# Dummy matmuls ahead of the first products, the first gate sum behind 40 of them, and a planner with longer DMA turns and a cold tensor clock

## The chip, the cores and the metric

The kernel runs on one core of a Trainium2 chip. The metric is the time of one execution in device microseconds. On one chip the runs of one kernel spread by one or two per cent (the kernel before: 189.54 to 192.09 us on the chip of the first experiments, 186.75 to 189.81 on that of the others), and two chips differ as well: its medians there were 191.5 and 188.7 us. Kernels are therefore compared as ratios to the kernel before of the same rounds on the same chip. A ratio is the mean time of one kernel's fast runs over that of the other's, with a 95% interval, so it is not quite the ratio of the medians that are quoted.

## The reference

```
def _attn_ref(q, k, v, f_logit):           # 4 batches, 8 heads, 768 steps, 48 wide
    f = 1.0 / (1.0 + np.exp(-f_logit))
    for t in range(S):
        state = f[:, :, t, :, None] * state + np.einsum('bhd,bhe->bhde', k[:, :, t], v[:, :, t])
        y[:, :, t] = np.einsum('bhd,bhde->bhe', q[:, :, t], state)

def _moe_ref(x, w_in, w_out):              # 3072 tokens, 384 -> 2048 -> 384
    h = x @ w_in
    g = h * np.cos(h)
    return g @ w_out
```

The rows of y, 3072 tokens by 384, are the x of the second part.

## The kernel before

The recurrence is cut into 24 chunks of 128 tokens. For each chunk four loads bring f, k, q and v. ACT makes the logarithm of the gate (sp), PE sums it over the chunk (the "gate sum"), ACT takes two exponentials of the sum (b and bi), DVE or POOL multiplies them into q and k (qk), PE or a DMA transposes the product (qkt), PE forms scores, DVE masks them (am), PE forms y, y is transposed to xT, and then the products with w_in, a cosine on ACT, a multiply on DVE and the output products with w_out follow.

All operations are put into a fixed order by a small planner that runs when the program is built. Each engine then works through its own list strictly in order. The planner's estimates (durations, priorities, turns of the DMA) decide only the order; at run time semaphores decide the times.

```
def chunk_load(b, c, prio):
    for pool, src in ((fS, f_logit), (kS, k), (qS, q), (vS, v)):
        way = QUEUES[min(b * NCH + c, len(QUEUES) - 1)][len(vals)]
        eng, dma = {"S": ({"SP": 650.0}, nc.sync), "A": ({"ACT": 600.0}, nc.scalar), ...}[way]
        P.op(eng, lambda e, ...: dma.dma_start(out=t.ap, in_=ap), writes=[t], ...)
...
P.op({"PE": 268.0}, pe, reads=[sp], writes=[pc], ...)        # the gate sum
P.op({"ACT": 385.0}, ex, reads=[pc], writes=[bt], ...)       # its two exponentials
P.op({"ACT": 385.0}, lambda e, ...: ex(e, pc, bi, 1.0, H * D), reads=[pc], writes=[bi], ...)
...
order = P.run()                                              # the plan
for o in order:
    o.fn(o.eng)                                              # the program, in that order
```

A load with the letter A is issued by ACT.

Of the kernel before, what the change touches and what calls it, by code (L numbers as in the profile page):

```python
# [96 lines left out]
class Plan:  # L97


    SEM = 80.0  # L100
    DMA = 1.048
    WAIT = {'PE': 0.0, 'ACT': 196.0, 'DVE': 108.0, 'POOL': 601.0}
    RING = 2600.0

    def __init__(self):
        self.ops = []
# [34 lines left out]
    def run(self):  # L141
        engs = ("PE", "ACT", "DVE", "POOL", "SP")
        free = dict.fromkeys(engs, 600.0)
        table, lock = "E", None

        ring, large = [0.0, 0.0], False
        left = {}
        for o in self.ops:
            o.waiting = len(o.deps)
            for d in o.deps:  # L150
                d.after.append(o)
            if o.grp is not None:
                left[o.grp] = left.get(o.grp, 0) + 1
        ready = [o for o in self.ops if not o.waiting]
        order = []
        n = len(self.ops)
        while len(order) < n:
            picks, first = [], {}
            for o in ready:
                at = max([d.end + (0.0 if e0 == d.eng == "PE" else self.SEM)  # L160
                          for d in o.deps for e0 in (next(iter(o.eng)),)], default=0.0)
                ok, took = True, []
                for v in o.alloc:
                    if v.slot is not None:
                        continue
                    b = v.pool.best()
                    if b is None:
                        ok = False
                        break
                    at = max(at, b[0] + self.SEM)  # L170
                    v.pool.take(b[1])
                    took.append((v.pool, b[1]))
                for pool, i in took:
                    pool.drop(i)
                if not ok:
                    continue
                pick = None
                for e, cost in o.eng.items():
                    if e == "ACT" and lock is not None and o.grp != lock and o.table is not None:
                        continue  # L180
                    s = max(at, free[e])
                    if o.dma and e != "POOL":
                        s = max(s, ring[0] - self.RING)
                    sw = 1300.0 if e == "ACT" and o.table not in (None, table) else 0.0
                    if pick is None or s + cost + sw < pick[0]:
                        pick = (s + cost + sw, s, e, cost)
                if pick is None:
                    continue
                picks.append((o.prio, o.seq, pick[1], o, pick[2], pick[3]))
                first[pick[2]] = min(first.get(pick[2], pick[1]), pick[1])  # L190

            best = {}
            for p in sorted(picks, key=lambda p: p[:2]):
                if p[4] not in best and p[2] <= first[p[4]] + self.WAIT.get(p[4], 0.0):
                    best[p[4]] = p
            assert best, "no op can be placed: " + str(
                [(o.seq, o.eng, o.prio, lock, o.grp, [v.pool.name for v in o.alloc]) for o in ready])
            _, _, s, o, e, cost = min(best.values(), key=lambda p: (p[2],) + p[:2])
            if e == "ACT" and o.table is not None:
                if o.table != table:  # L200
                    s += 1300.0
                table = o.table
                if o.grp is not None:
                    left[o.grp] -= 1
                    lock = o.grp if left[o.grp] else None
            for v in o.alloc:
                if v.slot is not None:
                    continue
                _, i = v.pool.best()
                v.slot = i  # L210
                v.pool.take(i)
            o.start, o.end = s, s + cost + o.lat
            if o.dma:
                q = int(e == "POOL")
                o.dma *= self.DMA
                t = max(ring[q], s + cost)
                both = max(0.0, ring[1 - q] - t)
                if q:
                    large = o.dma > 1500.0
                rate = (0.96 if q else 0.18) if large else 0.6  # L220
                if o.dma <= rate * both:
                    both = o.dma / rate
                    ring[q] = t + both
                else:
                    ring[q] = t + both + o.dma - rate * both
                ring[1 - q] += both * (1.0 - (0.18 if q else 0.96)) if large else 0.4 * both
                o.end = ring[q] + o.lat
            free[e] = s + cost
            o.eng, o.cost = e, cost
            if o.frees is not None:  # L230
                pool, i = o.frees
                pool.used(i, o.end)
                pool.drop(i)
            for v in o.vals:
                v.uses -= 1
                v.pool.used(v.slot, o.end)
                if not v.uses:
                    v.pool.drop(v.slot)
            ready.remove(o)
            for a in o.after:  # L240
                a.waiting -= 1
                if not a.waiting:
                    ready.append(a)
            order.append(o)
        order.sort(key=lambda o: (o.start, o.seq))
        return order
# [3 lines left out]
def kernel(  # L250
# [21 lines left out]


    GROUPS = [1, 1, 1, 1, 1, 1, 1, 1, 2, 2, 1, 1, 2, 3, 3, 1, 1]
    UNITS = [128, 128, 128, 128, 256, 128, 128, 128, 128, 256, 128, 128, 256, 256, 128, 128, 128, 128, 256]
    ATT = [31.5, -12.35, -0.91, -97.87, -9.39, -48.94, 43.41, -95.96, -1.09, -74.7, -11.15, -52.89, 4.11, -36.04, -25.81, 1.58, -156.13, -98.92, -140.35, -95.04, -72.72, -54.06, -183.38, -29.59]
    DEC = [10.57, -49.08, 3.05, 3.32, -36.4, -43.88, -42.65, -26.96, -17.74, -34.58, -18.58, -36.54, 0.15, -26.89, -9.76, -17.28, -17.13, -64.08, -49.12, -67.43, -2.25, -59.6, -104.93, -80.41]
    MM1 = [6.06, -27.94, -32.4, -100.05, -29.46, -56.23, -91.16, -82.46, -137.1, -25.66, -11.55, -122.15, -148.98, -96.28, -109.44, -65.59, -19.47, -6.91, 25.44, -46.31, -33.1, -47.12, -85.39, 1.66]
    MM2 = [13.76, 8.41, -13.19, 54.53, -13.62, -73.77, 64.32, 9.83, 51.7, 10.46, -31.46, 0.13, 11.13, 53.52, 21.21, 60.26, 109.18, 29.72, -36.43, 48.48, -26.47, -47.8, -64.39, -82.23]

    GATES = [2, 1, 1, 2, 2, 1, 2, 2]

    QUEUES = ["AAAS", "SAAA", "SSSS", "SSSS", "SSSS", "SSSS", "SSSS"]

    QK_DMA = [7, 10, 11, 12, 14, 15, 16, 17, 18, 19, 20, 21, 22, 23]
    X_DMA = [4, 7, 11, 12, 13, 14, 16, 19, 20, 21, 22]
    FAST = 16
    WARM = 0
    BUFS = {"ld": 8, "vb": 6, "sp": 6, "b": 6, "bi": 4, "qk": 5, "qkt": 7, "am": 5, "sz": 4, "y": 4, "st": 2, "co": 5, "ot": 5, "g": 4}
    CAPS = [6, 4, 3, 3, 3]  # L290

    cpool = ctx.enter_context(tc.tile_pool(name="const", bufs=1))
# [41 lines left out]
    phS = Banks(base, "ph", CAPS[1], [moe_cap])  # L334
# [7 lines left out]
    P = Plan()  # L342
# [4 lines left out]
    mk = Val()  # L347
    P.op({"POOL": 1100.0}, masks, writes=[mk], prio=-1.0)


    warm = Val(phS)
    for i in range(WARM):
        def idle(e):
            for _ in range(2):
                nc.tensor.matmul(warm.ap[:, 0:128], lhsT=ident, rhs=ident, start=True, stop=True)
        P.op({"PE": 220.0 if i < 16 else 112.0}, idle, reads=[mk], writes=[warm], prio=1e6)
    for pool, cost in zeroed:
        for i in range(len(pool.aps)):
            P.zero(pool, i, {"DVE": cost, "POOL": 2.0 * cost}, lambda e, t=pool.aps[i]: (
# [45 lines left out]
    def decay_group(chunks, g, prio):  # L405

        outs = []
        for (b, c, ld) in chunks:
            f = ld[0]
            sp = Val(spS)  # L410
# [13 lines left out]
        for (b, c, ld, sp) in outs:  # L424
            pc, bt, bi = Val(miS), Val(bS), Val(biS)
# [6 lines left out]
                                     lhsT=sp.ap[:, 2 * p:2 * p + 2, :].rearrange("p h d -> p (h d)"),  # L432
                                     rhs=umask[:, C - 1:C], start=False, stop=(p == NP - 1))

            P.op({"PE": 268.0}, pe, reads=[sp], writes=[pc], prio=prio, lat=170.0)

            def ex(e, pc=pc, o=bt, s=-1.0, n=H * D + NP):
                nc.scalar.activation(out=o.ap, in_=pc.ap[:, 0:n], func=AF.Exp, scale=s)  # L438
# [3 lines left out]
                 reads=[pc], writes=[bi], prio=prio, table="E", grp=g)  # L442
# [3 lines left out]
    def attend(b, c, ld, bt, bi, prio):  # L446
# [3 lines left out]
        qk = Val(qkS)  # L450
        half = lambda a, i: a[:, i * NP * C:(i + 1) * NP * C].rearrange(
            "p (h d) -> p h d", d=64)[:, :, 0:D]
        qtd = qk.part(lambda a: half(a, 0))
        ktd = qk.part(lambda a: half(a, 1))
        fast = tok < FAST * C
        E = lambda e: nc.vector if e == "DVE" else nc.gpsimd
        for src, w, dst in ((qf, bt, qtd), (kf, bi, ktd)):
# [7 lines left out]
             reads=[v32], writes=[vf], prio=prio)  # L465
# [24 lines left out]
                P.op({"DVE": 340.0, "ACT": 480.0}, evac, reads=[pqk], writes=[dst], prio=prio)  # L490
        else:
            P.op({"SP": 1000.0}, lambda e: nc.sync.dma_start_transpose(out=qkt.ap, in_=qk.ap),
                 reads=[qtd, ktd], writes=[qdt, kdt], prio=prio, lat=1250.0, dma=1400.0)


        pas, ams = [Val(paS), Val(paS)], [Val(amS), Val(amS)]
# [80 lines left out]
                 prio=prio)  # L577
        else:
            P.op({"SP": 700.0}, lambda e: nc.sync.dma_start_transpose(out=x.ap, in_=yt.ap),
                 reads=[yt], writes=[x], prio=prio, lat=1250.0, dma=480.0)  # L580


    def moe(u, t0, T):
# [113 lines left out]
```

## Time and profile before

| | before |
|---|---|
| median of the first 3 timed runs, us | 191.31 (190.42 to 191.63) |
| the profiled run, us (span) | 195.14 (193.4), slow |
| PE busy, share of the span | 172.3 us, 89% |

The prediction below shows and reads the page. The columns of the timeline are start, length, engine, line, operation, and in brackets the idle time just before with what ended it; "ACTq" is ACT's instruction queue.

```profile
8.32 0.52 ACT L416 ACTIVATE sp<-f 128x384 bf16<-128x384 f32 x1
9.89 0.49 ACT L438 ACTIVATE b<-ps 128x388 f32<-128x388 f32 x1 [1.05 <-PE ps L431]
10.28 0.48 ACT L438 ACTIVATE bi<-ps 128x384 f32<-128x384 f32 x1
10.94 0.38 ACTq L400 DMA_DIRECT2D v<-in_v_dram  x1
11.37 0.52 ACT L413 ACTIVATE f<-f 128x384 f32<-128x384 f32 x1 [0.60 <-DMA q<-in_q_dram]
```

The reader is to see that the second chunk's v load is issued by ACT at 10.94, after the exponentials of the second gate sum (L438), and that ACT stands idle for 0.6 us only.

### The profile page before, as it was taken

The numbers are of one execution on the slowest core, as the hardware profiler recorded it, in microseconds if no ns is written. First come the engines' busy times: TensorE is split into PE (matmuls) and PEld (weight loads), VectorE is DVE, ScalarE is ACT, GpSimd is POOL, SyncE is SP. The second block draws the span as 40 slices with busy tenths as digits, with TensorE's granted clock in tenths as the row PEclk, the third lists the DMA queues.
The fourth block names the chain that finished last, engine by engine and source line by source line (L and its number), as shares of the span: only waits on it lengthen the run. The fifth ranks groups of instructions, "written<-read, shape, count | busy, mean of one in ns | idle before, by whom it ended". The sixth has DMA issues, their size and how long they took to land.

```text
span 193.4 us, 5275 instructions
## 1 busy us (share of the span) xinstructions
PE 172.3 (89%) x2079; PEld 135.7 (70%) x2079; DVE 135.1 (70%) x254; ACT 139.8 (72%) x257; POOL 56.7 (29%) x97
## 2 busy tenths in 40 slices
PE   0378699999999999999499999969999999999991
PEld 0256599856886897866379666955879688987750
DVE  7287879936789996989837973956349948955200
ACT  3576589595999888989948399827879899735320
POOL 7007970112130331301140119810395183000000
PEclk9999789999999999999969999979999999999999
DMA  6999999969899799998796996997989666101041
GB/s 136 219 218 197 217 203 208 192 125 233 159 190 219 174 197 204 173 185 193 163 196 131 202 221 125 184 182 155 256 183 184 228 116 135 33 0 45 1 162 43
DMA packets 124858, 31.84 MB, mean 165 GB/s; under 512 B 119713, under 2 KB 124321, under 8 KB 124833
## 3 DMA queue, kind: packets, MB, share of 16 engines
q1 hardware_dynamic: 116416, 27.18, 70.7%
q0 software_dynamic: 2176, 3.15, 9.1%
q10 hardware_dynamic: 6240, 1.18, 3.7%
q8 instruction: 16, 0.26, 0.6%
q14 instruction: 10, 0.07, 0.2%
HBM read 25.17 MB, written 4.72 MB: 155 GB/s over the span
## 4 chain that ended last, share of the span: by engine, by line
PE 65%; DMA 13%; ACT 8%; DVE 5%; POOL 3%; issue 2%; SPq 2%; ACTq 1%; POOLq 0%
PE ps L598 26%; PE ps L620 24%; DMA qkt<-qk 5%; PE ps L501 4%; DVE gT L610 3%; DMA k<-in_k_dram 3%; PE ps L482 3%; DMA v<-in_v_dram 2%; DMA xT<-y 2%; PE ps L552 2%; PE ps L520 2%; PE ps L555 2%; PE ps L428 2%; SPq L400 1%; PE ps L573 1%
## 5 line engine op out<-in xcount | busy, mean ns | idle before, releaser
L598 PE MATMUL ps<-xT,w_in 128*128 128x128 bf16 (+1 forms) x912 | 73.3, 240 | 3.5 <-DMA xT<-y 3.1
L598 PEld LDWEIGHTS <-w_in 128*128 128x128 bf16 x912 | 67.6, 116 | 6.9 <-issue 3.3
L610 DVE TENSOR_TENSOR gT<-ps,cosh 128x512 bf16<-128x512 f32 x96 | 60.4, 683 | 14.9 <-ACT cosh L606 14.6
L620 PE MATMUL ps<-w_out,gT 128*128 128x384 bf16 x384 | 70.8, 328 | 0.0
L606 ACT ACTIVATE cosh<-ps 128x512 bf16<-128x512 f32 x96 | 54.5, 602 | 21.5 <-PE ps L598 18.7
L620 PEld LDWEIGHTS <-gT 128*128 128x128 bf16 x384 | 35.1, 98 | 19.8 <-issue 0.3
L508 DVE TENSOR_TENSOR am<-ps,umask 128x512 bf16<-128x512 f32 x48 | 30.6, 682 | 6.5 <-PE ps L501 6.2
L464 POOL CAST vb<-v 128x384 bf16<-128x384 f32 x24 | 13.1, 549 | 61.2 <-DMA v<-in_v_dram 37.0
L539 POOL TENSOR_TENSOR sz<-st,b 64x192 bf16<-64x192 f32 x32 | 16.1, 502 | 16.7 <-DVE st L535 13.9
L459 POOL TENSOR_TENSOR qk<-q,b 128x384 bf16<-128x384 f32 x12 | 12.1, 1005 | 26.1 <-ACT b L438 17.1
L535 DVE TENSOR_TENSOR st<-ps,sz 64x192 f32<-64x192 f32 x32 | 11.3, 353 | 9.3 <-PE ps L520 4.4
L438 ACT ACTIVATE b<-ps 128x388 f32<-128x388 f32 x24 | 11.9, 496 | 5.7 <-PE ps L431 4.4
L629 ACT COPY ot<-ps 128x384 f32<-128x384 f32 x19 | 9.0, 485 | 8.4 <-PE ps L620 8.1
L413 ACT ACTIVATE f<-f 128x384 f32<-128x384 f32 x24 | 12.5, 522 | 2.0 <-DMA f<-in_f_logit_dram 1.3
L428 PE MATMUL ps<-sp,umask 128*128 128x384 bf16 x24 | 8.4, 355 | 5.8 <-ACT sp L416 5.7
L562 ACT CAST y<-ps 128x384 bf16<-128x384 f32 x18 | 8.5, 478 | 6.9 <-PE ps L555 5.5
L416 ACT ACTIVATE sp<-f 128x384 bf16<-128x384 f32 x24 | 12.6, 524 | 0.7
L482 PE MATMUL ps<-ident,qk 128*128 128x128 bf16 x80 | 8.3, 246 | 4.9 <-DVE qk L459 4.9
L501 PE MATMUL ps<-qkt 48*128 48x128 bf16 x192 | 10.3, 233 | 2.1 <-DMA qkt<-qk 2.0
L459 DVE TENSOR_TENSOR qk<-k,bi 128x384 bf16<-128x384 f32 x16 | 9.8, 612 | 3.2 <-ACT bi L438 3.0
L438 ACT ACTIVATE bi<-ps 128x384 f32<-128x384 f32 x24 | 11.8, 493 | 0.0
L431 PEld LDWEIGHTS <-sp 128*128 128x128 bf16 x96 | 6.1, 100 | 6.6 <-issue 4.8
(39 smaller groups left out, 139.4 us busy)
## 6 DMA issues: line engine op xcount, KB each, us to landing
out_dram<-ot SPq DMA_DIRECT2D x24, 192.0 KB, 2.7
v<-in_v_dram SPq DMA_DIRECT2D x23, 192.0 KB, 4.6
f<-in_f_logit_dram SPq DMA_DIRECT2D x23, 192.0 KB, 4.2
k<-in_k_dram SPq DMA_DIRECT2D x22, 192.0 KB, 3.9
q<-in_q_dram SPq DMA_DIRECT2D x22, 192.0 KB, 4.5
w_in<-in_moe_w_in_dram POOLq DMA_DIRECT2D x4, 384.0 KB, 7.5
w_out<-in_moe_w_out_dram POOLq DMA_DIRECT2D x4, 384.0 KB, 10.4
k<-in_k_dram ACTq DMA_DIRECT2D x2, 192.0 KB, 5.3
```

The costliest lines, as they stand in the source:

```text
L416: nc.scalar.activation(out=sp.ap[:, :, 0:D], in_=f.ap, func=AF.Ln, bias=1.0)
L438: nc.scalar.activation(out=o.ap, in_=pc.ap[:, 0:n], func=AF.Exp, scale=s)
L459: lambda e, src=src, w=w, dst=dst: E(e).tensor_mul(out=dst.ap, in0=src.ap, in1=w.ap[:, 0:H * D].rearrange("p (h d) -> p h d", d=D)),
L464: o = P.op({"POOL": 510.0}, lambda e: nc.gpsimd.tensor_copy(out=vf.ap, in_=v32.ap), reads=[v32], writes=[vf], prio=prio)
L482: nc.tensor.transpose(out=o[:, i, :], in_=qk.ap[:, j * C:(j + 1) * C], identity=ident)
L501: nc.tensor.matmul(pas[g].ap[:, p * C:(p + 1) * C], lhsT=kdt.ap[64 * g:64 * g + D, p, :], rhs=qdt.ap[64 * g:64 * g + D, p, :], start=(p == ...
L508: nc.vector.tensor_mul(out=am.ap, in0=pa.ap.rearrange("p (a n) -> p a n", n=C), in1=umask[:, None, :].broadcast_to([128, 4, C]))
L539: o = P.op(cost, lambda e, g=g, srcap=srcap, out=out: E(e).tensor_mul(out=out.ap, in0=srcap(), in1=bt.ap[rows(g), H * D:, None].broadcast_ ...
L598: nc.tensor.matmul(ph.ap[:, g * T:(g + 1) * T], lhsT=w_in_bf[s0][:, m, f0::4], rhs=x[:, m, :], start=(g == 0 and m == 0), stop=(g == G - 1 ...
L606: P.op({"ACT": 490.0}, lambda e, ph=ph, co=co: nc.scalar.activation(out=co.ap, in_=ph.ap, func=AF.Sin, bias=HALF_PI), reads=[ph], writes=[ ...
L610: P.op({"DVE": 605.0}, lambda e, ph=ph, co=co, gv=gv: nc.vector.tensor_mul(out=gv.ap, in0=ph.ap.rearrange("p (g t) -> p g t", t=T), in1=co ...
L620: nc.tensor.matmul(po.ap[:, 0:d_model], lhsT=gT.ap[:, j, i * 128:(i + 1) * 128], rhs=w_out_bf[s][:, j - 4 * s, :], start=(j == 0), stop=(j ...
```

## The change

The intent is to keep TensorE busy, and so at its full clock, until the products begin, to let the planner know that PE is slow at first, and to bring weights and products forward. The diff, cut (priorities ATT, DEC, MM1 and MM2, the planner's waits and small constants are all set anew as well):

```
+    COLD = 8000.0
...
+            took = 2.0 * cost if e == "PE" and s < self.COLD else cost
...
-    GATES = [2, 1, 1, 2, 2, 1, 2, 2]
+    GATES = [0, 1, 2, 2, 3, 3, 2, 4]
-    QUEUES = ["AAAS", "SAAA", "SSSS", ...]
+    QUEUES = ["SAAS", "AAAA", "SSSS", ...]
-    QK_DMA = [7, 10, 11, 12, 14, 15, ...]          # 14 of them
+    QK_DMA = [7, 10, 11, 12, 15, ...]              # 13
-    X_DMA = [4, 7, 11, 12, 13, 14, 16, 19, 20, 21, 22]
+    X_DMA = [4, 7, 11, 13, 14, 16, 19, 21, 22]
-    WARM = 0
+    WARM = 90
...
     for i in range(WARM):                          # a pair of 128x128 matmuls each
-        P.op({"PE": 220.0 if i < 16 else 112.0}, idle, reads=[mk], writes=[warm], prio=1e6)
+        w = P.op({"PE": 110.0}, idle, reads=[mk], writes=[warm], prio=1e6)
+        if i < 20:
+            first_warm = w
...
+            o = P.op({"PE": 268.0}, pe, reads=[sp], writes=[pc], prio=prio, lat=170.0)
+            if g == 0:
+                o.deps.add(first_warm)             # first gate sum behind 20 pairs
...                                                # planned turns of the DMA transposes
-                 ... lat=1250.0, dma=1400.0)       # qkt
+                 ... lat=1250.0, dma=1600.0)
-                 ... lat=1250.0, dma=480.0)        # xT
+                 ... lat=1250.0, dma=750.0)
```

QUEUES now has all four loads of the second chunk on ACT. GATES lets the first w_in load start after the first v cast.

More of the change, by code (lines that the diff above doesn't have):

```diff
@@ L100 @@
     SEM = 80.0
-    DMA = 1.048
-    WAIT = {'PE': 0.0, 'ACT': 196.0, 'DVE': 108.0, 'POOL': 601.0}
+    DMA = 1.039
+    WAIT = {'PE': 18.0, 'ACT': 242.0, 'DVE': 73.0, 'POOL': 343.0}
     RING = 2600.0
+    COLD = 8000.0
     def __init__(self):
@@ L211, in run @@
                 v.pool.take(i)
-            o.start, o.end = s, s + cost + o.lat
+            took = 2.0 * cost if e == "PE" and s < self.COLD else cost
+            o.start, o.end = s, s + took + o.lat
             if o.dma:
@@ L227, in run @@
                 o.end = ring[q] + o.lat
-            free[e] = s + cost
+            free[e] = s + took
             o.eng, o.cost = e, cost
@@ L274 @@
     GROUPS = [1, 1, 1, 1, 1, 1, 1, 1, 2, 2, 1, 1, 2, 3, 3, 1, 1]
-    UNITS = [128, 128, 128, 128, 256, 128, 128, 128, 128, 256, 128, 128, 256, 256, 128, 128, 128, 128, 256]
-    ATT = [31.5, -12.35, -0.91, -97.87, -9.39, -48.94, 43.41, -95.96, -1.09, -74.7, -11.15, -52.89, 4.11, -36.04, -25.81, 1.58, -156.13, -98.92, -140.35, -95.04, -72.72, -54.06, -183.38, -29.59]
-    DEC = [10.57, -49.08, 3.05, 3.32, -36.4, -43.88, -42.65, -26.96, -17.74, -34.58, -18.58, -36.54, 0.15, -26.89, -9.76, -17.28, -17.13, -64.08, -49.12, -67.43, -2.25, -59.6, -104.93, -80.41]
@@ L278 @@
-    MM1 = [6.06, -27.94, -32.4, -100.05, -29.46, -56.23, -91.16, -82.46, -137.1, -25.66, -11.55, -122.15, -148.98, -96.28, -109.44, -65.59, -19.47, -6.91, 25.44, -46.31, -33.1, -47.12, -85.39, 1.66]
-    MM2 = [13.76, 8.41, -13.19, 54.53, -13.62, -73.77, 64.32, 9.83, 51.7, 10.46, -31.46, 0.13, 11.13, 53.52, 21.21, 60.26, 109.18, 29.72, -36.43, 48.48, -26.47, -47.8, -64.39, -82.23]
-    GATES = [2, 1, 1, 2, 2, 1, 2, 2]
-    QUEUES = ["AAAS", "SAAA", "SSSS", "SSSS", "SSSS", "SSSS", "SSSS"]
-    QK_DMA = [7, 10, 11, 12, 14, 15, 16, 17, 18, 19, 20, 21, 22, 23]
@@ L286 @@
-    X_DMA = [4, 7, 11, 12, 13, 14, 16, 19, 20, 21, 22]
+    UNITS = [128, 128, 128, 128, 256, 128, 128, 128, 128, 256, 128, 128, 256, 256, 128, 128, 128, 128, 128, 128]
+    ATT = [39.89, -60.87, -14.09, -112.01, -41.72, -49.81, 26.57, -83.74, -7.26, -76.0, -17.9, -58.25, -33.27, -35.47, -31.92, 0.04, -144.3, -98.01, -163.35, -118.29, -77.77, -79.02, -204.85, -70.45]
+    DEC = [2.02, -61.8, 0.77, 4.29, -41.77, -55.76, -37.45, -19.44, -18.02, -35.35, -9.18, -30.14, 16.98, -3.25, 1.47, 1.7, -5.21, -33.59, -25.76, -33.88, 24.21, -31.31, -85.07, -50.55]
@@ new lines @@
+    MM1 = [0.79, -34.63, -40.47, -103.67, -68.47, -68.15, -103.65, -92.07, -142.06, -54.25, -47.86, -195.21, -178.56, -123.33, -158.12, -119.16, -37.61, -14.65, 29.7, 35.98, -44.37, -39.81, -68.47, -80.46]
+    MM2 = [16.4, 12.31, 5.91, 68.78, -6.18, -74.16, 32.99, 14.3, 31.73, 7.84, -10.91, -0.02, 41.88, 40.44, 30.64, 108.56, 140.44, 32.08, -56.82, -38.73, 47.2, -23.95, -57.2, -83.05]
+    GATES = [0, 1, 2, 2, 3, 3, 2, 4]
+    QUEUES = ["SAAS", "AAAA", "SSSS", "SSSS", "SSSS", "SSSS", "SSSS"]
+    QK_DMA = [7, 10, 11, 12, 15, 16, 17, 18, 19, 20, 21, 22, 23]
@@ L287 @@
+    X_DMA = [4, 7, 11, 13, 14, 16, 19, 21, 22]
     FAST = 16
-    WARM = 0
-    BUFS = {"ld": 8, "vb": 6, "sp": 6, "b": 6, "bi": 4, "qk": 5, "qkt": 7, "am": 5, "sz": 4, "y": 4, "st": 2, "co": 5, "ot": 5, "g": 4}
+    WARM = 90
+    BUFS = {"ld": 8, "vb": 6, "sp": 6, "b": 5, "bi": 4, "qk": 5, "qkt": 7, "am": 5, "sz": 4, "y": 4, "st": 3, "co": 5, "ot": 5, "g": 4}
     CAPS = [6, 4, 3, 3, 3]
@@ L348 @@
     P.op({"POOL": 1100.0}, masks, writes=[mk], prio=-1.0)
-    warm = Val(phS)
+    warm, first_warm = Val(phS), None
     for i in range(WARM):
@@ L433, in pe @@
                                      rhs=umask[:, C - 1:C], start=False, stop=(p == NP - 1))
-            P.op({"PE": 268.0}, pe, reads=[sp], writes=[pc], prio=prio, lat=170.0)
+            o = P.op({"PE": 268.0}, pe, reads=[sp], writes=[pc], prio=prio, lat=170.0)
+            if g == 0:
+                o.deps.add(first_warm)
             def ex(e, pc=pc, o=bt, s=-1.0, n=H * D + NP):
@@ L492, in attend @@
             P.op({"SP": 1000.0}, lambda e: nc.sync.dma_start_transpose(out=qkt.ap, in_=qk.ap),
-                 reads=[qtd, ktd], writes=[qdt, kdt], prio=prio, lat=1250.0, dma=1400.0)
+                 reads=[qtd, ktd], writes=[qdt, kdt], prio=prio, lat=1250.0, dma=1600.0)
         pas, ams = [Val(paS), Val(paS)], [Val(amS), Val(amS)]
@@ L579, in attend @@
             P.op({"SP": 700.0}, lambda e: nc.sync.dma_start_transpose(out=x.ap, in_=yt.ap),
-                 reads=[yt], writes=[x], prio=prio, lat=1250.0, dma=480.0)
+                 reads=[yt], writes=[x], prio=prio, lat=1250.0, dma=750.0)
     def moe(u, t0, T):
```

## The prediction

> **What bounds the kernel now.** I read the page first. TensorE is busy in nearly every slice after the opening, while no other engine and not the DMA is:
>
> ```profile
> span 193.4 us, 5275 instructions
> PE 172.3 (89%) x2079; PEld 135.7 (70%) x2079; DVE 135.1 (70%) x254; ACT 139.8 (72%) x257; POOL 56.7 (29%) x97
> ...
> PE   0378699999999999999499999969999999999991
> ...
> PEclk9999789999999999999969999979999999999999
> ```
>
> The reader is to see three weak places in the PE row: slices 1 to 5 (0 to 24 us), slice 20 (92 to 97 us) and slice 27 (126 to 131 us). Second I read the chain of waits in order of time, for the price of matmuls and for what filled the weak places (columns: start, length, what):
>
> ```profile
> 8.53 0.61 PE ps L482 x4
> ...
> 15.90 0.92 PE ps L482 x8
> ...
> 23.99 2.13 PE ps L598 x24
> ...
> 28.89 5.36 PE ps L598 x96
> ...
> 37.07 0.65 PE ps L620 x4
> ...
> 92.36 4.46 DMA xT<-y
> 96.87 4.45 PE ps L598 x24
> ...
> 121.89 5.53 DMA qkt<-qk
> ...
> 127.86 2.63 PE ps L598 x24
> ...
> 171.59 2.62 PE ps L598 x24
> ```
>
> Warm, a 128-column matmul costs 5.36/96 = 56 ns, a 384-column one 0.65/4 = 162 ns, a 256-column one 2.62/24 = 109 ns (171.59). Cold, 128 columns cost 0.92/8 = 115 ns (15.90), and the 256-column ones after the wait at 92.36 cost 4.45/24 = 185 ns. Third, the busy time by stage (length, then PE, PEld, DVE, ACT, POOL, with counts, then granted clock, DMA, GB/s):
>
> ```profile
> 10.00:15.00 5.00, 3.90 (x41) 2.60 (x41) 4.11 (x9) 3.89 (x9) 0.70 (x1) 1.00 1.40 218
> 15.00:20.00 5.00, 3.75 (x43) 2.96 (x43) 3.70 (x9) 3.80 (x9) 3.80 (x7) 1.00 1.24 193
> 20.00:25.00 5.00, 4.08 (x56) 3.41 (x57) 4.52 (x10) 2.84 (x7) 3.90 (x7) 0.71 1.25 223
> ```
>
> In the opening DVE, ACT and the DMA (around 200 GB/s, its highest) are all nearly full, so PE is not alone there.
>
> From these prices I made a ledger. I priced every matmul of the instruction order warm (a gate sum 0.27 us, four transposes 0.22, eight scores 0.33, twelve products 0.67, four output matmuls 0.65) and compared the sum ahead of each gate sum (line 428) with the time at which the timeline starts that gate sum. The whole kernel is 158.4 us of warm PE work. Lost up to the 5th gate sum: 23.1 - 6.3 = 16.8 us; up to the 6th: 42.0 - 23.9 = 18.1; 16th: 93.8 - 73.6 = 20.2; 17th: 114.5 - 89.5 = 25.0; 20th: 137.0 - 107.4 = 29.6; 24th: 157.2 - 127.3 = 29.9. So the loss is 18 us in the opening and two steps of about 4.7 us each in the middle; the rest runs at PE's pace. Each step is a wait for a DMA transpose (2.7 us for xT, 1.8 us for qkt in the timeline) followed by cold matmuls. One caution: this profiled run took 195.14 us and is marked slow; the timed median is 191.31, so a typical run loses some 4 us less, probably in these two steps.
>
> **What the Trainium skill says.** "TensorE: Matmul & The Clock Gate", Part 1: the array runs at half clock until it has been busy for a window of about 3.4 us, and falls back after an idle window; it gives 107 ns cold and 56 ns warm at 128 columns. The trace agrees (115 and 56). The same page, Seeing it yourself, warns that the recorded clock events are not to be trusted; the trace agrees: the recorded clock is 1.00 from 10 to 20 us, where the transposes run cold. So I judge the clock by matmul spacing. "ScalarE: Activation LUTs", What ACT_TABLE_LOAD costs: 1283 ns plus a drain of 1380 ns. The trace has the 1283, but the next activation starts at once (load at 111.98 for 1.28 us, exponential at 113.28), so I count 1.3 us. "DMA: Bandwidth & Descriptors", Issuing engines are not separate DMA queues: all queues share the same 16 engines. So weights fetched earlier delay chunk loads; the full DMA of the opening agrees.
>
> **The change part by part.**
>
> (1) Dummies and the clock. 180 dummy matmuls (90 pairs) are added; 40 stand ahead of the first gate sum. The masks are ready at 1.87 us; 40 cold ones at 107 to 115 ns take 4.3 to 4.6 us, so the first gate sum can start at 6.2 to 6.5 us instead of 5.74. That costs about nothing: in the old trace ACT takes the gate sum's exponential only at 7.00, because its queue is held at 6.43 by the issue of a load. From then on PE is warm. On the opening chain there are some 15 short PE pieces (transposes, scores, y); four transposes take 0.61 cold and 0.40 warm including latency, so I estimate 0.2 us each, 3 us in all, less what DVE and ACT take back, since they are 75 to 90% full there.
>
> (2) Weights and first products. The order shows the first w_in load straight after the first v cast (old cast at 4.2 us, its first w_in at 15.7). With issue to landing as measured,
>
> ```profile
> w_in<-in_moe_w_in_dram POOLq DMA_DIRECT2D x4, 384.0 KB, 7.5
> ...
> qkt<-qk SPq DMA_TRANSPOSE x14, 3.9
> xT<-y SPq DMA_TRANSPOSE x11, 3.0
> ```
>
> it lands at about 13 us, and following the new DVE order (multiplies 0.56, copies 0.42, masks 0.68, y 0.55) the first chunk's xT is there at about 14 us. So the first 12 products start near 14 instead of 23.8. But only 12: the next gate sum (the 4th) waits for ACT to load the sine table, do one cosine, and load the exponential table back, 1.3 + 0.6 + 1.3 = 3.2 us (two extra pairs of table loads in all: 10 and 9 instead of 8 and 7). I get the 4th gate sum at about 18.2 (18.8 before) and the last dummy right after it. Then products need the second w_in, issued after the second v cast at about 14 us, landing near 22. By then 6.8 us of warm work are done. From there PE should be full, with ACT's cosines pacing it closely. Lost at that point: 22 - 6.8 = 15.2, plus about 0.4 of small waits = 15.6, against 18.1. Gain 2.5 us.
>
> (3) The middle. The planner's price for a qkt transpose goes from 1000 + 1400 x 1.048 + 1250 = 3.7 us to 1000 + 1600 x 1.039 + 1250 = 3.9 us, the measured 3.9; for xT from 2.45 to 2.73, nearer to 3.0. One qkt and two xT transposes move to PE. At the first step (xT of the 12th chunk) the warm work between y and the first product goes only from 5.07 to 5.30 us: this wait stays. At the second step (qkt of the 19th chunk) the work between gate sum and scores goes from 10.9 to 12.3 us, 1.4 more against a wait of 1.8: this wait nearly vanishes and its cold matmuls with it, up to 4.4 us in the profiled run. As typical runs lose 4 us less, I count half: 2.2 us.
>
> (4) More PE work: the last 256-token unit becomes two of 128: 96 x 56 - 48 x 109 = +0.1 us; 8 + 6 more transposes at 56 ns = +0.8. Sum +0.9. The end stays 48 output matmuls, an eviction (0.48) and a store (2.7).
>
> Sum: 191.3 - 2.5 - 2.2 + 0.9 = 187.5 us.
>
> **The rivals.** (a) Weights arrive on time and the clock does the rest: products run unbroken from about 19 us, the loss falls to 13, and with (3) the time is about 185. For it: load latencies were never below PE's need once products ran. Against it: DMA already full. (b) The early weights starve the chunk loads and the early table switches hold the gate sums, while dummies sit in order ahead of late work: the opening gains nothing, and the 0.9 us remains: about 190 to 191. For it: ACT at 3.8 of 5 us and DVE at 4.1 of 5 in the opening. Against it: PE's cold pieces lie on the chain itself. (c) The waits for transposes only move: chunk 22's xT slack falls from 6.8 to 4.1 us of work; a new wait there with a cold stretch costs 2 to 4 us and gives (3) back: about 190. Against it: chunk 19 had 3.7 and no wait was seen there.
>
> **Range and chances.** Both gains certain in sign to me but not in size: 184.2 to 191.0 holds it 8 times in 10. The mark for faster is 191.31 x 0.98 = 187.5, right on my value: 0.48 faster, 0.48 same, 0.04 slower.
>
> **What would show it.** Right if four transposes take about 0.4 us from 8 us on, if products start near 14, if PE is full from about 22, if the 6th gate sum's loss is 15 to 16.5, if a wait for xT remains near 90 us and that for qkt near 125 is gone. Wrong if PE idles on w_in between 19 and 25 us for more than 3 us, if the 4th gate sum comes after 19 us, or if new transpose waits appear in the second half.

## The result

| | before | after |
|---|---|---|
| median, us | 191.34 (190.42 to 191.63), 4 runs | 194.03 (193.53 to 194.46), 4 runs |
| ratio | | 1.0148 [1.0106, 1.019] |
| profiled run, us | 195.14 (slow) | 194.46 |

The changed kernel is 1.5% slower (by the 2% mark still "same"), and 6.5 us above the predicted 187.5. It is outside the predicted range. The record does not name the chip of this result. The head of its page:

```profile
span 192.4 us, 5765 instructions
## 1 busy us (share of the span) xinstructions
PE 179.1 (93%) x2321; PEld 145.2 (76%) x2321; DVE 140.6 (73%) x267; ACT 140.8 (73%) x253; POOL 56.8 (30%) x96
...
PE   7843999999999999999999999998999999989992
...
ACT  3404469897799987999899768996999896742510
```

The two weak slices in the middle (20 and 27 of the PE row) are gone. What is left is one hole, in slices 3 and 4 (about 10 to 19 us), and the ACT row has a 0 at the same place. The busy time by stage (length, then PE, PEld, DVE, ACT and POOL with counts, granted clock, DMA share, GB/s) makes it plain; the second and third stretch were shown of the kernel before:

```profile
5.00:10.00 5.00, 4.46 (x68) 3.95 (x68) 2.20 (x5) 2.16 (x5) 1.38 (x2) 1.00 1.41 218
10.00:15.00 5.00, 1.97 (x36) 1.69 (x34) 1.08 (x3) 0.00 (x0) 0.00 (x0) 1.00 1.27 222
15.00:20.00 5.00, 2.39 (x29) 2.23 (x30) 2.37 (x5) 2.68 (x6) 0.04 (x1) 0.68 0.94 187
```

From 10 to 15 us ACT does nothing at all, where it was busy for 3.89 of 5 us before. PE fell from 3.90 to 1.97 there. The timeline of ACT says what ended the idle time:

```profile
8.43 0.52 ACT L421 ACTIVATE sp<-f 128x384 bf16<-128x384 f32 x1
15.66 0.37 ACTq L405 DMA_DIRECT2D v<-in_v_dram  x1
16.08 0.49 ACT L445 ACTIVATE b<-ps 128x388 f32<-128x388 f32 x1 [7.14 <-DMA v<-in_v_dram]
```

ACT stood idle for 7.14 us ahead of the exponential of the second gate sum, which needs no v. (The second gate sum is that of the third chunk here; the plan takes the gate whose f comes first.) What stood between was the issue of the second chunk's v load, and it was released by the landing of another v load. The chain of waits (start, length, what) has both ends, and what came after:

```profile
6.21 9.44 DMA v<-in_v_dram
15.64 0.02 issue
15.66 0.37 ACTq L405
...
16.48 0.49 ACT bi L445
16.97 0.02 issue
16.99 0.57 DVE qk L466
17.56 0.04 issue
17.61 0.61 PE ps L489 x4
18.21 0.32 PE ps L433
...
18.62 0.24 PE ps L358 x2
18.86 0.32 PE ps L559 x8
19.18 1.71 PE ps L358 x16
20.88 0.32 PE ps L580 x3
21.20 0.64 PE ps L358 x6
...
23.12 0.99 PE ps L605 x12
```

A v load issued at 6.21 by SP, the third chunk's, landed at 15.64, and only then could ACT issue the second chunk's v. The exponentials, the multiply, the transposes (L489) and the next gate sum (L433) followed. Since PE's list is in order, even the first chunk's y (L559), its transpose to xT (L580) and the first products (L605) waited behind them, until 23. The pieces of L358 are dummies: with those at 22.27 (not shown), 28 of them stand ahead of the first products here, at the half clock, for 3.0 us.

The program as built explains the odd partner. These are the loads in ACT's and SP's lists up to the two in question, with the semaphore on which each issue waits (chunks counted from 1):

```
changed kernel   ACT: k1, q1, f2, k2 [waits 0], q2 [waits 2], v2 [waits 1]
                 SP:  f1, v1, f3, k3, q3, v3 [waits 1], ...
before           ACT: f1, k1, q1, k2, q2 [waits 2], v2 [waits 7]
                 SP:  v1, f2, f3, k3, q3, v3 [waits 1], ...
```

Semaphore 1 goes from f1 to v3, and from v3 to v2. The second chunk's v thus waits for the third chunk's v, which is queued behind much else. In the kernel before it got semaphore 7, which the third chunk's q had, and that landed just as ACT came to the issue.

The prediction's ledger (the start of a gate sum less the warm PE work ahead of it, dummies not counted as work) gives the sizes. The 6th gate sum of the changed kernel starts at 46.81, with 23.0 us of warm work ahead: 23.8 us lost, against 18.1 before and 15.6 predicted. The 24th loses 27.7, so 3.9 us were lost between the two.

### The profile page after: what moved, and what is told of

The parts are those of the page before. It is cut to its first block, busy times and chain, and to the rows that moved or that the text cites. A ratio compares the mean times of both kernels' runs of the same rounds, so it can differ in the third digit from the quotient of the medians.

```text
span 192.4 us, 5765 instructions
## 1 busy us (share of the span) xinstructions
PE 179.1 (93%) x2321; PEld 145.2 (76%) x2321; DVE 140.6 (73%) x267; ACT 140.8 (73%) x253; POOL 56.8 (30%) x96
## 4 chain that ended last, share of the span: by engine, by line
PE 63%; DMA 12%; SPq 8%; DVE 7%; issue 3%; POOL 3%; ACT 1%; ACTq 0%; DVEq 0%; POOLq 0%
PE ps L627 25%; PE ps L605 24%; SPq L405 8%; DMA v<-in_v_dram 5%; DMA qkt<-qk 3%; PE ps L489 2%; PE ps L508 2%; DVE am L515 2%; DVE qk L466 2%; DMA xT<-y 2%; PE ps L559 2%; POOL qk L466 2%; DMA k<-in_k_dram 2%; PE ps L433 2%; PE ps L358 2%
## 5 line engine op out<-in xcount | busy, mean ns | idle before, releaser
L605 PE MATMUL ps<-xT,w_in 128*128 128x128 bf16 (+1 forms) x960 | 69.7, 231 | 1.1 <-DMA xT<-y 0.8
L627 PE MATMUL ps<-w_out,gT 128*128 128x384 bf16 x384 | 69.5, 326 | 0.0
L605 PEld LDWEIGHTS <-w_in 128*128 128x128 bf16 x960 | 65.6, 114 | 3.2 <-DMA xT<-y 1.2
L613 ACT ACTIVATE cosh<-ps 128x512 bf16<-128x512 f32 x96 | 53.9, 604 | 9.8 <-PE ps L605 6.4
L627 PEld LDWEIGHTS <-gT 128*128 128x128 bf16 x384 | 34.9, 98 | 20.4
L546 POOL TENSOR_TENSOR sz<-st,b 64x192 bf16<-64x192 f32 x32 | 16.8, 525 | 39.0 <-DVE st L542 33.8
L358 PE MATMUL ps<-ident 128*128 128x128 bf16 x180 | 16.3, 257 | 1.4 <-POOL ident masks.py:199 1.4
L636 ACT COPY ot<-ps 128x384 f32<-128x384 f32 x16 | 7.6, 478 | 11.2 <-PE ps L627 11.1
L358 PEld LDWEIGHTS <-ident 128*128 128x128 bf16 x180 | 13.8, 118 | 1.7 <-POOL ident masks.py:199 1.4
L489 PE MATMUL ps<-ident,qk 128*128 128x128 bf16 x88 | 8.7, 232 | 6.6 <-DVE qk L466 6.2
L613 ACT ACT_TABLE_LOAD x10 | 12.8, 1283 | 0.2
L466 DVE TENSOR_TENSOR qk<-q,b 128x384 bf16<-128x384 f32 x15 | 8.3, 553 | 5.7 <-ACT b L445 5.6
L489 PEld LDWEIGHTS <-qk 128*128 128x128 bf16 x88 | 6.2, 104 | 7.7 <-DVE qk L466 6.5
```

What stands on the lines that cost most here:

```text
L358: nc.tensor.matmul(warm.ap[:, 0:128], lhsT=ident, rhs=ident, start=True, stop=True)
L466: lambda e, src=src, w=w, dst=dst: E(e).tensor_mul(out=dst.ap, in0=src.ap, in1=w.ap[:, 0:H * D].rearrange("p (h d) -> p h d", d=D)),
L489: nc.tensor.transpose(out=o[:, i, :], in_=qk.ap[:, j * C:(j + 1) * C], identity=ident)
L546: o = P.op(cost, lambda e, g=g, srcap=srcap, out=out: E(e).tensor_mul(out=out.ap, in0=srcap(), in1=bt.ap[rows(g), H * D:, None].broadcast_ ...
L605: nc.tensor.matmul(ph.ap[:, g * T:(g + 1) * T], lhsT=w_in_bf[s0][:, m, f0::4], rhs=x[:, m, :], start=(g == 0 and m == 0), stop=(g == G - 1 ...
L613: P.op({"ACT": 490.0}, lambda e, ph=ph, co=co: nc.scalar.activation(out=co.ap, in_=ph.ap, func=AF.Sin, bias=HALF_PI), reads=[ph], writes=[ ...
```

## The experiments

Three theories were to be told apart. The first, which the expectations call H2, is the held queue: ACT's list is blocked by the issue of one load. The rivals are that the early w_in load delays the chunk loads (PE, DVE and ACT starve for data), and that the dummies stand in PE's order ahead of real work. In all but one experiment the plan of its base kernel was left as it was and only the named operations were moved or left out when the program was put together, so that the order of everything else stayed the same. The times that the expectations name for the first four runs on the second chip fit the pace of the first one, so for these the ratios are the better guide.

The first four ran on one chip (before: median 191.49, 189.54 to 192.09), all others on a second (before: 188.7).

**v1_early.** The second chunk's v load is issued from ACT's list straight after its f load, ahead of all its own activations.

```
 order = P.run()
+at = {o.tag: o for o in order if o.tag}
+order.remove(at[('v', 1)])
+order.insert(order.index(at[('f', 1)]) + 1, at[('v', 1)])
```

> The changed kernel's plan, frozen, with one load's issue moved: the second chunk's v is issued by ACT right after its f (near 4 us) and not after the second gate's softplus (near 9 us). Theory H (ACT's queue is held for 7.1 us, from 8.95 to 15.66, by the issue of this load, which waits for a semaphore that an earlier load still holds): the hold goes, the third gate sum starts at 11 to 13 us and not 18.0, the loss at the 6th gate sum falls from 23.8 to 17 to 19, the time falls by 4 to 6.5 us to 187.5 to 190. Rival D (dummies in order ahead of real work make the opening long): within 1 us of 194.0. Rival W (the weights fetched early take the DMA from the chunk loads, and the data itself comes late): a fall of at most 2 us, with ACT waiting for f, k or q data instead.

Measured: 190.65 us (189.7 to 191.58), ratio 0.9967 [0.9883, 1.0052]. The hold is gone and some 1.8% of the time with it (0.9967 against 1.0148 with the hold, two chips). The loss at the 6th gate sum was 19.5, so it fell by 4.3 of the 5.7 us that had been added. The expectation was missed a little (time 187.5 to 190, loss 17 to 19), and by more for the third gate sum, which ran at 15.13 and not at 11 to 13. Another load paid: the second chunk's q, now last of its four, was issued at 7.32 and landed 10.29 us later, as the chain of this run has it:

```profile
7.32 10.29 DMA q<-in_q_dram
```

The second v cast, by the timeline of POOL, came early:

```profile
10.05 0.58 POOL L473 CAST vb<-v 128x384 bf16<-128x384 f32 x1 [2.65 <-DMA v<-in_v_dram]
```

**no_dummies.** All 180 dummies are left out of the program; the plan is unchanged.

```
-            o.fn(o.eng)
+            if o.prio < 1e6:
+                o.fn(o.eng)
```

> The changed kernel's plan, frozen, with none of the 180 dummy matmuls issued. Theory H: the hold of ACT stays at about 7 us and the third gate sum stays near 18 us, the time within 1.5 us of 194.0 and rather longer, as the pieces of the opening run cold. Rival D: 2 us or more faster, 192 or below, third gate sum well before 18.

Measured: 191.0 us (187.7 to 191.53). Three of the four runs were slow, being over 1.5% above the fastest, so no ratio was formed. The profiled run took 187.7 us, with a loss of 18.3 at the 6th gate sum and no hold. The program shows why it left: without the dummies the second chunk's v load waits on semaphore 6, used by the second chunk's own f, which lands early. By the marks of the expectation the time fell on the rival's side (192 or below), and the forecast that the hold would stay was wrong. The dummies are not loads and use none of these semaphores, yet which semaphore a load is given depends on whether they are there. This made this experiment ambiguous: it takes away the dummies and the hold at once. The runs forty_dummies, no_first_forty and load_before_gate were made to separate them.

**w_later.** The first w_in load goes back behind the second v cast.

```
+order.remove(at[('w', 0)])
+order.insert(order.index(at[('cast', 1)]) + 1, at[('w', 0)])
```

> The changed kernel's plan, frozen, with the first w_in load issued after the second v cast and not after the first. ACT's queue still waits for the same semaphore. If the early weight load is what makes the load that holds it land after 9.4 us, that load lands in 5 to 6 us, the hold shrinks from 7.1 to 2 to 3.5 us, the loss at the 6th gate sum falls by 2 to 4 us and the time to 190 to 192. If the early load is not the cause of the late landing, the hold stays at 6 us or more and the time is 194 or longer, since the first products come later.

Measured: 199.37 us (196.6 to 200.96), ratio 1.0376 [1.027, 1.0483]. The third chunk's v landed at 12.74 instead of 15.64, as its chain shows in "6.08 6.66 DMA v", so the hold fell from 7.1 to 4.4 us. The early weights do delay the loads. But the expectation was missed (hold 2 to 3.5, time 190 to 192): the products, planned for early weights, waited on PE:

```profile
PE ps L608 <- DMA w_in<-in_moe_w_in_dram: 5.9, 1, 5.9
```

(columns: total us, times, longest). The early weights lengthen the hold, but they are also needed by the order that was planned around them.

**before_w_early.** The reverse, in the kernel before: one w_in load is moved up to just after the first v cast.

```
+order.remove(at[('w', 1)])
+order.insert(order.index(at[('cast', 0)]) + 1, at[('w', 1)])
```

> The kernel before, its plan frozen, with its first w_in load moved up to right after the first v cast. Converse of the last run. Theory H with the early weights as its root: ACT's issue of the second chunk's v (0.38 us at 10.94, no hold in the kernel before) or of an earlier load is now held, by 2 to 5 us, and the time rises by 2 to 4 us to 193 to 195. If early weights do no harm: within 1 us of 191.3.

Measured: 193.43 us (191.1 to 193.8), ratio 1.0089 [1.0003, 1.0174]. The loss at the 6th gate sum rose from 18.1 to 20.4. The timeline of ACT shows a hold of the same kind (v2 behind q3, which comes later now), 3.08 us where it was 0.60:

```profile
13.40 0.38 ACTq L401 DMA_DIRECT2D v<-in_v_dram  x1
13.82 0.52 ACT L415 ACTIVATE f<-f 128x384 f32<-128x384 f32 x1 [3.08 <-DMA q<-in_q_dram]
```

So early weights cost the opening of this kernel about 2 us in all. How much of that came through the queue of ACT was not separated.

**forty_dummies and no_first_forty.** The first keeps only the 40 dummies ahead of the first gate sum, the second only the 140 after it; plan unchanged.

```
+    dropped = {id(w) for i, w in enumerate(dummies) if not (i < 20)}    # forty_dummies
+    dropped = {id(w) for i, w in enumerate(dummies) if not (i >= 20)}   # no_first_forty
-            o.fn(o.eng)
+            if id(o) not in dropped:
+                o.fn(o.eng)
```

> The changed kernel's plan, frozen, with only the 40 dummies ahead of the first gate sum issued, the other 140 left out. In the program as built the second chunk's v load then still waits for the same semaphore as in the changed kernel (number 1, held by the third chunk's v). Theory H2 (the semaphore that the load is given decides; dummies matter by shifting that choice): hold of ACT of 6 to 8 us, third gate sum at 17.5 to 18.5, time 193 to 195. Rival D2 (the dummies themselves, as work in order on PE, cost the 3 us that leaving all of them out gained): most of the dummies are gone, so 191 to 192 and no hold.

> The changed kernel's plan, frozen, with the first 40 dummies left out and the other 140 kept. As built, the load then waits for semaphore number 6 (held by the second chunk's f, which lands early). H2: no hold (under 1 us), third gate sum at 12 to 13, loss at the 6th gate sum 17.5 to 18.5, time 187.5 to 191. D2: 140 of 180 dummies are still in order on PE, so 193 to 194.

In the built programs the first keeps semaphore 1 for the load in question and the second gives it semaphore 6. Measured: forty_dummies 191.65 us (191.19 to 192.53), ratio 1.0179 [1.0085, 1.0273]; no_first_forty 187.28 us (186.18 to 187.61), ratio 0.9936 [0.9861, 1.0012]. They ran on one chip and differ by 4.4 us, with no run of one within the times of the other. (The 191.65 us is in the range that the expectation gives to the rival D2, but on a faster chip; what tells D2 from H2 is which of the two is slow, and that the hold is there.) The version with fewer dummies of the two is the slow one. In it, the waits of ACT (columns as above) have the hold:

```profile
ACT b L447 <- DMA v<-in_v_dram: 6.1, 1, 6.1
```

In no_first_forty the same part of ACT's timeline is

```profile
8.22 0.43 ACTq L407 DMA_DIRECT2D v<-in_v_dram  x1
9.27 0.49 ACT L447 ACTIVATE b<-ps 128x388 f32<-128x388 f32 x1 [0.54 <-PE ps L438]
```

the load goes out at once, and ACT works on at 9.27 instead of 16.08. From 10 to 15 us PE is full, 5.00 of 5, and the first products come where the prediction had put them:

```profile
14.46 0.83 PE L607 MATMUL ps<-xT,w_in 128*128 128x128 bf16 x12
17.14 0.33 PE L529 MATMUL ps<-vb,qk 128*128 128x96 bf16 x4 [1.84 <-POOL vb L473]
```

at 14.46. But then PE waits for the cast of the second chunk's v (L473), 48 dummies follow in its list, and the 4th gate sum comes at 23.38, not at the predicted 18.2. The loss at the 6th is 18.6, no better than before's 18.1.

**load_before_gate.** All 180 dummies stay, and the second chunk's v load is moved four places up in ACT's list, ahead of the first chunk's exponentials.

```
+load, act = at['v', 1], [o for o in order if o.eng == "ACT"]
+to = act[act.index(load) - 4]
+order.remove(load)
+order.insert(order.index(to), load)
```

> All 180 dummies kept, plan frozen, the load moved four places up on ACT, to just ahead of the first exponential of a gate sum; as built it then waits for semaphore number 4 (held by the third chunk's f). H2: hold under 1.5 us, third gate sum at 12 to 14, and with PE warm the loss at the 6th gate sum is 16 to 18.5, time 187 to 191. If dummies are harmful by themselves the time stays at 193 or above without a hold.

Measured: 188.3 us (187.8 to 189.63), ratio 1.0012 [0.9931, 1.0093]; loss at the 6th gate sum 18.7. The load now waits on semaphore 4, of the third chunk's f, which landed at 7.29. The issue goes out at once after that, but takes 1.39 us itself, and the first exponentials start at 8.74 instead of 7.11, 1.6 us later:

```profile
7.30 1.39 ACTq L406 DMA_DIRECT2D v<-in_v_dram  x1
8.74 0.49 ACT L447 ACTIVATE b<-ps 128x388 f32<-128x388 f32 x1 [3.52 <-issue]
```

The hold and the loss were expected a little lower (under 1.5 and 16 to 18.5), and the third gate sum at 12 to 14; it ran at 15.20. Here the dummies do stand in the way: the multiply was done at 13.68, and the transposes (L492) came only at 14.98, after 28 dummies that had begun at 12.36 and took 94 ns each, most of them cold. Still, with every dummy in place the time goes back to that of the kernel before, once the long hold is gone: what the dummies delay on the way does not show in the total.

**v1_on_sp.** One letter: QUEUES "AAAA" becomes "AAAS". Here the planner planned anew.

> The changed kernel with one letter changed: the second chunk's v goes through SP's queue and not ACT's, and the planner makes a new plan. No load with a late semaphore is left on ACT. H2: no hold, loss at the 6th gate sum 16 to 18.5; the rest of the plan is new, so the time is less certain, 187 to 191. If the early weights alone were the trouble (rival W) it stays at 193 or above with waits for f, k or q data.

Measured: 207.22 us (205.76 to 211.03), ratio 1.098 [1.0878, 1.1081]: a plain miss. The hold is gone, but with one load on another engine the planner's order changed everywhere, with priorities that were tuned for another order. The largest wait of PE in this run shows a new place:

```profile
PE ps L508 <- ACT qkt L495: 5.3, 1, 5.3
```

This run says nothing about the hold. It says that in this kernel an experiment has to keep the plan.

**before_again.** The kernel before, one look with a profile, since its first profile was a slow run.

> The kernel before, unchanged, for a profile in its usual state. If typical runs lose less in the two transposition waits of the middle, as the prediction assumed from the slow profile (195.1 us), the loss between the 6th and the 24th gate sum is 7 to 8.5 us here and not 11.8, and the loss up to the 6th gate sum is again 17.5 to 18.5.

Measured: 187.79 us, one run, on the second chip, its state unknown. The loss was 18.1 at the 6th gate sum, as in the slow profile, but only 22.6 at the 24th: 4.5 us in between, where 7 to 8.5 were expected. PE's waits in the slow profile of before were

```profile
PE ps L598 <- DMA xT<-y: 3.1, 2, 2.7
PE ps L501 <- DMA qkt<-qk: 2.0, 2, 1.8
```

and here, in the order of size, were

```profile
PE ps L428 <- ACT sp L416: 5.7, 1, 5.7
PE ps L482 <- DVE qk L459: 4.8, 5, 2.2
PE ps L573 <- ACT y L562: 0.6, 1, 0.6
PE ps L428 <- ACT ot L629: 0.5, 1, 0.5
```

No wait for a DMA transpose appears. The two steps of 4.7 us in the middle, on which part of the prediction was built, are not in this run.

**small_w0.** no_first_forty with the first w_in load cut to a third of its bytes, the rest of that tile set to zero on DVE. Its output is wrong, which doesn't matter for the time.

```
+    nc.vector.memset(dst.ap[:, 1:KM, :], 0.0)
+    nc.gpsimd.dma_start(out=dst.ap[:, 0:1, :], in_=src[:, 0:1, :])
```

> The kernel without the first forty dummies (no hold), with its first w_in load cut to a third of its bytes, the rest of that tile zeroed; the result is wrong on purpose. Theory W2 (the opening is bound by the DMA: the early weights only push the chunk loads back, so the second chunk's v lands at 16.6 and not at 13.5 as predicted): its cast comes at 13 to 15, the 4th gate sum at 19 to 21.5 and not 23.4, the loss at the 6th gate sum is 16 to 17.8 and not 18.6. Rival C (the order of PE and the table loads of ACT bound the opening): cast earlier or not, the 4th gate sum stays at 22.5 to 23.5 and the loss within 0.5 of 18.6.

Measured: 187.2 us (185.32 to 187.88), ratio 0.9926 [0.9836, 1.0017]. The second v cast, as the timelines of POOL have it in no_first_forty

```profile
16.59 0.50 POOL L473 CAST vb<-v 128x384 bf16<-128x384 f32 x1 [9.26 <-DMA v<-in_v_dram]
```

and in small_w0

```profile
14.47 0.50 POOL L478 CAST vb<-v 128x384 bf16<-128x384 f32 x1 [7.11 <-DMA v<-in_v_dram]
```

came 2.1 us earlier with a third of the bytes, close to the predicted 14. The loss at the 6th gate sum fell from 18.6 to 16.7. The zeroing on DVE is not free: the third gate sum ran at 13.40, against 11.82 without it. In the total nothing is to be seen beyond the noise: the 24th lost 22.3, against 21.7 in no_first_forty.

**best_again and no_dummies_again.** The best version so far (the changed plan with the first forty dummies left out, the same edit as no_first_forty) and the version without any, five rounds each, on one chip.

> The kernel without the first forty dummies, again, five rounds: 0.5 to 1% faster than the kernel before.

> The plan of the changed kernel without any dummy, again, on the same chip as the last. Neither has the hold; they differ in 140 dummies, that is in a warm clock in the opening. If the warm clock is worth what the prediction said (about 3 us before what DVE and ACT take back), this one is 1.5 to 3 us slower than the last; if the opening waits for data and not for PE, within 0.7 us of it.

Measured: best_again 187.65 us (186.84 to 188.56), ratio 0.9967 [0.9899, 1.0036]; no_dummies_again 187.79 us (186.66 to 189.12), ratio 0.9973 [0.9906, 1.004]. The 140 dummies that keep the clock up are worth 0.1 us, which is nothing within the spread, where 1.5 to 3 us would have borne the prediction out. Neither version is shown to be faster than the kernel before (0.5 to 1% had been expected of best_again). Both are about 1.8% better than the changed kernel (0.997 against 1.0148, on different chips).

In sum, with the loss at the 6th gate sum and what was lost from there to the 24th, both in us and from the one profiled run of each kernel (v1_on_sp is left out, as its order is another). The third column is the idle time of ACT at the issue of v2; where it says 1.6, it is how much later than in the changed kernel the first exponentials started. The hold of 1.3 to 1.75 us ahead of these by the issue of q2, which the other runs have, is not counted:

| run | semaphore of v2 | ACT held by an issue | loss at 6th | 6th to 24th | ratio |
|---|---|---|---|---|---|
| before (slow profile) | 7 | 0.6 | 18.1 | 11.8 | 1 |
| before_again | 7 | 0.6 | 18.1 | 4.5 | none formed |
| before_w_early | 7 | 3.1 | 20.4 | 5.3 | 1.0089 |
| after | 1 | 7.1 | 23.8 | 3.9 | 1.0148 |
| forty_dummies | 1 | 6.1 | 22.3 | 4.1 | 1.0179 |
| w_later | 1 | 4.4 | 26.0 | 7.1 | 1.0376 |
| load_before_gate | 4 | 1.6 | 18.7 | 3.2 | 1.0012 |
| v1_early | 0 | 1.6, by q2 | 19.5 | 4.8 | 0.9967 |
| no_first_forty | 6 | none | 18.6 | 3.1 | 0.9936 |
| best_again | 6 | none | 18.2 | 3.9 | 0.9967 |
| no_dummies | 6 | none | 18.3 | 3.5 | none formed |
| no_dummies_again | 6 | none | 17.7 | 3.3 | 0.9973 |
| small_w0 | 6 | none | 16.7 | 5.6 | 0.9926 |

## Why the prediction was wrong

**The step that failed** is in part (2) of the working: "following the new DVE order (multiplies 0.56, copies 0.42, masks 0.68, y 0.55) the first chunk's xT is there at about 14 us", and with it "I get the 4th gate sum at about 18.2". It added the durations of the work and took ACT to be free. ACT was held for 7.1 us by the issue of a load, so the first products came at 22.9 instead of 14 and the 4th gate sum at 28.60. Without the hold the latter came at 23.38 (no_first_forty) and 23.39 (load_before_gate), so 5.2 of the 10.4 us by which it was late are the hold's; the rest belongs to the second term below and to the dummies (21.2 and 21.4 in the two runs without any, 22.0 and 23.38 in those with the later 140). The prediction's own mark for an error, a 4th gate sum after 19 us, was passed. Without the hold the first products came at 14.46 in no_first_forty, so up to there the working on DVE and PE was sound and the missing term was the queue of ACT. With all the dummies and the load moved (load_before_gate) they came at 18.06: there the first exponentials were 1.6 us late, and the 28 dummies ran mostly cold. The prediction had even seen such a hold, of 1.3 us ahead of the first chunk's exponentials ("its queue is held at 6.43 by the issue of a load"), and used it to excuse the dummies; it did not ask what the issue was waiting for, nor what all four loads of the second chunk on ACT would then do.

**The sum.** At the 6th gate sum 15.6 us of loss were predicted and 23.8 came, 8.2 more. Of these, the hold is 5.1 to 5.6 (23.8 less 18.7 in load_before_gate, 18.6 and 18.2 in the two runs of the version without the first forty). The other 2.6 to 3.1 are a second term that was mis-sized: the DMA's. The second v cast, which was to price the second weight load, was predicted at 14 and came at 16.6 even without the hold (19.96 with it), because the early w_in load pushes the chunk loads back (small_w0 gets 1.5 to 1.9 us of the loss back; in the kernel before, the same early load costs 2.3). But the cast alone is not the limit: in v1_early it came at 10.05 and the second w_in landed at 18.42, 5 us before that of no_first_forty, and yet the loss was 19.5, since now q landed late. What makes up the last 1 us or so is not shown. In the middle, the prediction implied 11.8 - 3.8 (the slow profile against the median) - 2.2 = 5.8 us lost between the 6th and the 24th, and 3.9 were lost: 1.9 better. 8.2 - 1.9 = 6.3, of the 6.5 us by which the time was missed.

**Point by point.** The first gate sum was put at 6.2 to 6.5 and ran at 5.61. Four transposes were to take 0.4 us from 8 us on:

```profile
5.61 0.53 PE L433 MATMUL ps<-sp,umask 128*128 128x384 bf16 x1
8.25 0.40 PE L489 MATMUL ps<-ident,qk 128*128 128x128 bf16 x4 [0.54 <-DVE qk L466]
17.61 0.61 PE L489 MATMUL ps<-ident,qk 128*128 128x128 bf16 x4 [5.63 <-DVE qk L466]
```

They did at 8.25, but at 17.61, after 5.6 us of idling, they took 0.61 again. The dummies can't bridge such a hole, as they stand in PE's list behind the transposes that wait. The estimate that the warm clock gives 3 us in the opening (no term of the sum was built on it) was wrong too: with 140 dummies or with none, the loss at the 6th gate sum is 18.2 to 18.6 and 17.7 to 18.3, and the times agree within 0.1 us. Without dummies PE is busy for only 2.86 of the 5 us from 10 to 15, and no more is lost: its pace is not what the opening waits for.

A wait for xT near 90 us was to remain and did not; that for qkt near 125 was to vanish and did. PE's waits for transposes in the changed kernel are

```profile
PE ps L605 <- DMA xT<-y: 0.8, 1, 0.8
PE ps L508 <- DMA qkt<-qk: 0.6, 1, 0.6
```

They stand at 169.67 and 133.27, both in the second half, where new ones were named as a sign of being wrong; but they are small. Whether the loss of the two old waits is a gain of the change over a usual run of before is not shown: before_again, on the second chip, had neither wait, and lost 4.5 us there against 3.9; on the chip of the result no usual run of before was profiled, and the slow profile less the 3.8 us to the median gives an estimate of 8.0. The caution in the prediction about the slow profile was right. The 0.9 us of added PE work is in the program as counted; no run isolates it. Rival (b), early weights that starve the chunk loads, has a part of the truth (before_w_early, small_w0), but its 190 to 191 us is what the versions without the hold show (0.994 to 1.001 of 191.3), not this kernel. The hold was in none of the rivals.

**What stays open.** Why the builder's turn through the eight semaphores moves with the dummies was not followed into the builder; the lists of the built programs show only that it does: by the numbers, v2 takes its turn after the fifth chunk's k in the changed kernel and after the fourth chunk's q in no_first_forty, though the order of the loads in each engine's list is the same. The held issue also made v2 itself land late (19.90, against 16.53 and 16.73 in no_first_forty and load_before_gate); what of the 5.1 to 5.6 us is due to that and what to the standstill of the activations was not separated. That other opening orders could gain more from the warm clock was not tried.

## What to carry to other kernels

An issue of a load stands in the list of the engine that issues it, with whatever wait it carries, so a load on ACT is a possible stop of all activations behind it: put it early in the list (v1_early and load_before_gate, at 0.997 and 1.001, though other loads or exponentials then came later) or on an engine without compute (which no run here shows to pay), and read in the built program which semaphore it waits on and who signals that. Operations that have nothing to do with loads can change this choice, so after adding or removing some, look again; and an experiment that drops them may remove something else with them. A stage's new time is the latest of all engines' lists, not the sum of durations on the one that was to be sped up.

## What the Trainium skill lacked or had wrong

- "DMA: Bandwidth & Descriptors", Issuing engines are not separate DMA queues: it says that issuing from several engines only saves the sequencer's time, usually small beside the DMA. The issue itself was often small here too (0.37 us for the load in question), but not always: 1.39 us for the same load in load_before_gate, and up to 2.99 us for SP's loads in the changed kernel before 20 us. And spreading loads over SP and ACT couples the engines' lists: ACT stood still for 7.1 us, because its load's issue waited for a load of SP. The page does not warn of this, and the runs price it at about 4.4 us of 188 (forty_dummies against no_first_forty).
- None of the pages looked up tells that the built program shares eight completion semaphores among the loads of SP and ACT in turn, or that matmuls elsewhere change a load's number (1 with the first 40 or all 180 dummies, 6 with none or only the later 140).
- "TensorE: Matmul & The Clock Gate", Part 1, has the clock right (40 dummies from a cold start at 1.37 us to the gate sum at 5.61: 106 ns each, against the page's 107). What these runs add is that dummies which share PE's list with real work can't keep the clock up through a wait of that work: after 5.6 us of idling four transposes took 0.61 us again, with dummies left in the list.
- "ScalarE: Activation LUTs", What ACT_TABLE_LOAD costs: the 1283 ns are in the profile of the changed kernel as well (10 loads, 12.8 us), the drain of 1380 ns is not: in no_first_forty a copy ends at 14.14, a table load starts at 14.16 for 1.28 us and the cosine at 15.45.
